# Linear attention in a four-layer kernel: the third layer sums keys with normalised rows over the tokens and applies the value weights to the sums

## The chip, the core and the metric

The kernel runs on one core of one Trainium2 chip. Its time is in device microseconds (us), the median of three runs. The core has five engines with an instruction queue each: TensorE (PE, matrix products; its weight loads are listed as PEld), VectorE (DVE), ScalarE (ACT), GpSimd (POOL) and SyncE (SP). They share a memory of 128 partitions on the chip. Matrix products end in PSUM, eight banks of 128 partitions x 512 float32. DMA moves data to and from DRAM; in this kernel SP issues all of them.

## What is computed

The input x has 2048 tokens of 576 numbers (bfloat16). Two kinds of layer alternate, A, B, A, B, each as x = x + layer(layernorm(x)):

```python
def _A_ref(x, wqkv, wo):                      # x is already normalised
    B, S, D = x.shape                         # 1, 2048, 576
    H = 32; Dh = D // H                       # 18
    qkv = (x @ wqkv).reshape(B, S, 3, H, Dh).transpose(2, 0, 3, 1, 4)
    q, k, v = qkv[0], qkv[1], qkv[2]
    phi = lambda t: jnp.where(t > 0, t + 1, jnp.exp(t)) + 1e-6
    pq, pk = phi(q), phi(k)
    kv = jnp.einsum("bhsd,bhse->bhde", pk, v)
    z = jnp.einsum("bhsd->bhd", pk)
    num = jnp.einsum("bhqd,bhde->bhqe", pq, kv)
    den = jnp.einsum("bhqd,bhd->bhq", pq, z)[..., None] + 1e-6
    return (num / den).transpose(0, 2, 1, 3).reshape(B, S, D) @ wo

def _B_ref(x, w1, b1, w2, b2):                # x is already normalised
    y = _layernorm(x)
    h = gelu(y @ w1 + b1)                     # 4608 hidden
    return h @ w2 + b2
```

The kernel normalises once ahead of each layer. Layer 3 is the second A; the change is made there.

## The kernel before

**Tiles.** A *token tile* t is 128 tokens (16 of them, `NT`); a *chunk* c is four token tiles (`TPC` = 4, `CA` = 512 tokens, four chunks). The 576 columns are cut into five pieces of 128 (`KD`, the last of 64) where they are contracted, into five groups g of seven heads (126, 126, 126, 126, 72; `GR`, offsets `GO`) where heads matter, and into two halves of 288 (`HALF`). `yT` holds the normalised rows transposed, the columns on the partitions, for all tokens.

**Buffers.** `ps_h` has four PSUM buffers of one bank that nearly everything rotates through (keys, queries, denominators, h of the MLP); `ps_acc` has two of two banks, tags `accA` and `accB`. `blk` has 36 buffers of 128 x 576 bfloat16 for keys, queries, the hidden blocks `hT` of the MLP and more; `rows` has nine for rows of x in float32. `v_ring` is a ring of two value tiles.

**Order.** A helper `pe()` (L141) chains the products of TensorE in the order of the program. The other engines' queues are laid out by a scheduler, which some calls bind with `add_manual_dep` (one instruction not before another on the same queue). `warm_pe(n)` (L174) issues n products over zeros at the start (n = 11 at L812, 2 more at L822), while the first rows of x arrive and are normalised.

**Rows on their way into layer 3.** Layer 2 is an MLP; for its last chunk (as for each) 36 blocks hT are multiplied with w2 for one token tile after the other (L790). After each tile `residual` (L448) adds the layer's input and stores x to DRAM (`x_d`), and `LNPipe` (L264) normalises the tile in steps, one step per call of `tick`. With `evac="dma"` the normalised tile y is turned by `turn_rows` (L227): VectorE transposes blocks of 32 x 32 into `turned`, and after the fourth tile of a chunk SP stores them to `y_d` in DRAM in four pieces. `land` (L242) loads the chunk from `y_d` into `yT` some ticks later.

**Layer 3, the loop over tokens** (`layer_A`, L472, with li = 2; loop at L538). For each token tile: `k_proj` (L478) makes two halves of keys, five products of 288 columns each, into `k_ps`. The first half goes through `phi_from_psum` (L416: exp and an identity pass with bias 1 on ScalarE, then min/add and max on VectorE), the second through `phi_by_dve` (L407: exp on ScalarE, the rest on VectorE). `v_proj` (L493) makes the values in ten products (252 and 324 columns), which ScalarE and VectorE copy into `v_ring`; a column of ones stands beside them. `kv_acc` (L516) multiplies keys and values of the tile before, per group, five products of 126 (once 72) columns that are summed over all tokens in one PSUM buffer (`kvacc`). From the third tile on, one `q_proj` (L527; five products of 512 columns, then phi) follows: 16 of the 20 pairs (g, chunk) of queries are made in A.

**Layer 3, after the loop.** The sums are masked per head into `kvT` (L557, L561); z comes from the row of ones with five small products (L567) and is spread into `zsel` (L569, L571). Then the order is written out (L635 to L676): `kv_wo(g)` (L576) multiplies kvT of a group with wo, two products of 288 columns, copied out by ScalarE for even g, by VectorE for odd g; `den_stage(c)` (L591) sums the denominators of a chunk and takes the reciprocal; `quad_stage(c)` (L606) masks it for four token tiles; `scale_stage(g, c)` (L615) broadcasts it with one product of 512 columns (`rden_ps`), copied by ScalarE (`rden_bc`) and multiplied into pq by VectorE (L620); `wo_stage(t)` (L623) makes the output of a token tile with ten products of 288 columns and adds the residual. The order is kv_wo(0), a query, den 0, den 1, two queries around kv_wo(1), three scales, kv_wo(2) and (3), two scales, kv_wo(4), the last query; then the loop over t with, between the output tiles, the scales of the next chunk and the denominators of the one after.

**Layer 2's end.** `LayerB.run` (L758) walks the chunks; the last chunk's last tile (t = 15) is where the hidden blocks in `blk` come free for the last time before layer 3. Layers 1 and 4 are not touched but for the start-up and some memory set in layer 1.

Of the kernel before, what the change touches and what calls it, by code (L numbers as in the profile page):

```python
# [20 lines left out]
G = 5  # L21
# [13 lines left out]
def build(tc, A_x, A_wqkv, A_wo, B_w1, B_b1, B_w2, B_b2, out, dbg=None, n_layers=4):  # L35
    nc = tc.nc
    dbg = dbg or {}
    with ExitStack() as ctx:
# [76 lines left out]
        x_d = dpool.tile([NT, P, D], F32, name="x_d")  # L115
        y_d = [dpool.tile([D // 32, 32, CB], BF16, name=f"y_d{i}") for i in range(2)]
# [109 lines left out]

        def turn_rows(y, t, kind):  # L227
# [14 lines left out]
        def land(now=False):  # L242

            for it in list(landing):
# [8 lines left out]
                for hi in range(2 if kind == "B" else 1):  # L253
                    nc.sync.dma_start(out=yT[64 * hi:64 * (hi + 1), KD - 1, cols],
                                      in_=home[16:18, :, :].rearrange("jj r n -> (jj r) n"))

# [7 lines left out]
        class LNPipe:  # L264
# [11 lines left out]
            def tick(self, transposes=1):  # L276
                land()
                for it in list(self.items):
# [61 lines left out]
                    elif st in (2, 3):  # L340
# [18 lines left out]
                        if it["kind"] == "B" and it["evac"] != "dma":  # L359
                            nc.gpsimd.tensor_copy(out=y[:, D:DPAD], in_=y[:, 4 * P:D])  # L360
                        it["y"] = y
# [54 lines left out]
        def phi_from_psum(ps_ap, out_ap, rows, n, turned_cols=False):  # L416
# [3 lines left out]
            if turned_cols:  # L420
                e_out, a_out, ps_ap = spread(e_out), spread(a_out), gather(ps_ap)
            act_last["exp"] = nc.scalar.activation(out=e_out, in_=ps_ap, func=ACT.Exp).ins.name  # L422
            act_last["phi"] = nc.scalar.activation(out=a_out, in_=ps_ap, func=ACT.Identity, bias=C1,
                                                   scale=1.0).ins.name
            nc.vector.tensor_scalar(out=e[0:rows, 0:n], in0=e[0:rows, 0:n], scalar1=1.0, scalar2=1e-6,
                                    op0=ALU.min, op1=ALU.add)
            top = nc.vector.tensor_tensor(out=out_ap, in0=a[0:rows, 0:n], in1=e[0:rows, 0:n], op=ALU.max)
            dve_last["phi"] = top.ins.name
# [43 lines left out]
        def layer_A(li, next_kind, pre_a1=None):  # L472
# [54 lines left out]
            def q_proj(g, c):  # L527
# [6 lines left out]
                phi_from_psum(qp[0:GR[g], :], pq[(g, c)][0:GR[g], 0:CA], GR[g], CA, turned_cols=(li > 0))  # L534
# [3 lines left out]
            for t in range(NT):  # L538
# [13 lines left out]
            q_proj(*q_left.pop(0))  # L552
            kv_acc(NT - 1)
            q_proj(*q_left.pop(0))

            kvacc = kvacc_of["ps"]
            nc.vector.tensor_tensor(  # L557
                out=kvT[0:127, 0:4, :].rearrange("p g (h e) -> p g h e", h=7),
                in0=kvacc[0:127, 0, 0:504].rearrange("p (g h e) -> p g h e", g=4, h=7),
                in1=maskz[0:127, :, :].unsqueeze(1).to_broadcast([127, 4, 7, DH]), op=ALU.mult)  # L560
            nc.vector.tensor_tensor(  # L561
                out=kvT[0:127, 4, 0:72].rearrange("p (h e) -> p h e", h=4),
                in0=kvacc[0:127, 1, 0:72].rearrange("p (h e) -> p h e", h=4),
                in1=maskz[0:127, 0:4, :], op=ALU.mult)
            zp = ps_h.tile([P, 512], F32, name="z_ps", tag="h")
            for g in range(G):
                pe(nc.tensor.matmul(zp[0:GR[g], g:g + 1], lhsT=kvT[0:127, g, 0:GR[g]], rhs=z_row[0:127, :],  # L567
                                 start=True, stop=True))
# [5 lines left out]
            kvwo = {}  # L574

            def kv_wo(g):  # L576
                wp = ps_acc.tile([P, 2, 512], F32, name="kvwo_ps", tag=("accB", "accA")[g % 2])
# [5 lines left out]
                if g % 2:  # L583
                    nc.vector.tensor_copy(out=out, in_=wp[0:GR[g], :, 0:HALF])
                else:
                    nc.scalar.copy(out=out, in_=wp[0:GR[g], :, 0:HALF])
# [4 lines left out]
            def den_stage(c):  # L591
# [10 lines left out]
                with nc.allow_low_precision("reciprocal of the denominator in the reference's bfloat16"):  # L602
                    nc.vector.reciprocal(out=rden[:], in_=dp[:, 0:P])
                rden_of[c] = rden

            def quad_stage(c, after=None):  # L606
# [6 lines left out]
                quad_rden[c] = quad  # L613

            def scale_stage(g, c):  # L615
# [4 lines left out]
                nc.vector.tensor_tensor(out=pq[(g, c)][0:GR[g], 0:CA], in0=pq[(g, c)][0:GR[g], 0:CA],  # L620
                                        in1=rb[0:GR[g], 0:CA], op=ALU.mult)
# [26 lines left out]
            for g in range(3):  # L648
                scale_stage(g, 0)
# [257 lines left out]
```

## Time and profile before

| what | value |
| --- | --- |
| median of three runs | 774.79 us (774.26 to 775.12) |
| the profiled execution | 775.07 us, of it span 773.4 us |
| granted TensorE clock over the span | 1.00 |
| DMA, mean over the span | 88 GB/s; 30.0% of the engines' time |
| layer 3: first key product to end of output | 390.56 to 488.38 us |

The span runs from the first to the last instruction on the core. Costliest in layer 3 are the groups below: the line, engine, operation, output <- inputs, shapes and count; then the busy time in all, the mean duration of one in ns, and the idle time of the engine just before them with what ended it.

| group, 390.56 to 488.38 us | busy us | mean ns |
| --- | --- | --- |
| L530 PE q_ps, 512 columns, x100 | 25.0 | 382 |
| L484 PE k_ps, 288 columns, x160 | 22.2 | 286 |
| L628 PE wo_ps, 288 columns, x160 | 22.0 | 286 |
| L503 PE v_ps, 324 columns, x80 | 13.6 | 300 |
| L500 PE v_ps, 252 columns, x80 | 11.2 | 271 |
| L524 PE kvacc, 126 columns (and 72), x80 | 6.8 | 214 |
| L422 ACT exp of q_ps, x20 | 11.9 | 596 |
| L505 ACT copy v_ring<-v_ps, x16 | 9.3 | 579 |
| L620 DVE pq<-pq,rden_bc, x20 | 8.0 | 420 |
| L603 DVE reciprocal rden<-den_ps, x4 | 3.8 | 953 |

The duration of a product runs from its start to its modelled end, with the drain; consecutive products overlap, so durations add up to more than the time they take, and the step from start to start is the price of one more.

### The profile page before, as it was taken

The page shows a single profiled execution, that of the slowest core. Times are in us where ns is not written, and L with a number is a line of the kernel's source. Part 1 is how long each engine was busy: PE and PEld are TensorE (multiplying, and loading weights), DVE is VectorE, ACT ScalarE, POOL GpSimd, SP SyncE. Part 2 cuts the span into 40 slices and gives each one's busy share as a digit, 9 for nine tenths or more (in the row PEclk, how much of TensorE's full clock was granted, in tenths as well). Part 3 has the DMA queues.
Part 4 walks back from the last instruction along what each step waited for, and adds up shares of the span by engine and source line. Part 5 has one row for each costly group of instructions (what it writes and reads, how often), then busy time and mean ns, then how long its engine had stood idle before and what let it go on. Part 6 is the DMA issues. An engine that isn't in the chain of part 4 may idle for free.

```text
span 773.4 us, 15771 instructions
## 1 busy us (share of the span) xinstructions
PE 764.4 (99%) x6611; PEld 495.4 (64%) x6611; DVE 272.1 (35%) x685; ACT 345.4 (45%) x765; POOL 118.2 (15%) x191
## 2 busy tenths in 40 slices
PE   9999999999999999999999999999999999999998
PEld 6776664675477457646777766547745764675476
DVE  7786864036013503401355578520140032000000
ACT  5887946304610650264046677561065026304600
POOL 4571412013000301200100004110030012002000
PEclk9999999999999999999999999999999999999999
DMA  8991473016301710320440005830141033011000
GB/s 266 265 291 45 151 254 87 22 59 169 83 16 47 200 50 32 90 66 16 139 108 2 1 2 165 296 81 8 32 129 53 16 124 81 8 32 54 1 9 23
DMA packets 73761, 69.10 MB, mean 89 GB/s; under 512 B 34266, under 2 KB 58330, under 8 KB 73690
## 3 DMA queue, kind: packets, MB, share of 16 engines
q1 hardware_dynamic: 73690, 68.10, 30.0%
q8 instruction: 51, 0.84, 0.4%
q14 instruction: 20, 0.16, 0.1%
HBM read 45.67 MB, written 22.41 MB: 88 GB/s over the span
## 4 chain that ended last, share of the span: by engine, by line
PE 94%; DVE 2%; ACT 1%; DMA 1%; issue 1%; POOL 1%; SPq 0%; POOLq 0%; ACTq 0%; DVEq 0%
PE m_ps L790 35%; PE h_ps L736 20%; PE hp_ps L736 16%; PE q_ps L530 6%; PE k_ps L484 4%; PE wo_ps L628 3%; PE v_ps L503 2%; PE v_ps L500 2%; PE m_half L790 1%; PE kvacc L524 1%; PE tp L379 1%; PE rden_ps L617 1%; DMA x<-in_A_x_dram 1%; ACT rden_bc L619 1%; DMA xo<-x_d 0%
## 5 line engine op out<-in xcount | busy, mean ns | idle before, releaser
L790 PE MATMUL m_ps<-w_sb,hT 128*128 128x288 bf16 x2232 | 274.8, 286 | 0.0
L790 PEld LDWEIGHTS <-hT 128*128 128x128 bf16 x2304 | 224.8, 98 | 59.8 <-issue 3.4
L736 PEld LDWEIGHTS <-w_sb 64*128 64x128 bf16 x2304 | 124.6, 94 | 136.5 <-issue 1.9
L736 PE MATMUL hp_ps<-yT,w_sb 64*128 64x512 bf16 x1152 | 178.0, 376 | 0.0
L736 PE MATMUL h_ps<-yT,w_sb 64*128 64x512 bf16 x1152 | 148.0, 376 | 0.0
L741 ACT COPY relay_sb<-relay_sb 128x1 f32<-128x1 f32 x144 | 28.6, 198 | 262.3 <-PE h_ps L736 220.0
L732 ACT ACTIVATE hT<-h_ps,b1T 128x512 bf16<-128x512 f32 x144 | 91.1, 684 | 44.4 <-PE h_ps L736 44.4
L333 POOL TENSOR_TENSOR ln_rstd<-ln_u,neg_half 128x1 f32<-128x1 f32 x64 | 36.4, 570 | 385.0 <-DVE ln_u L324 241.1
L732 ACT ACTIVATE hT<-hp_ps,b1T 128x512 bf16<-128x512 f32 x144 | 91.2, 693 | 0.0
L462 DVE TENSOR_TENSOR xbf<-m_ps,xo 128x576 bf16<-128x576 f32 x15 | 11.4, 758 | 211.7 <-PE m_ps L790 211.7
L462 DVE TENSOR_TENSOR xo<-m_ps,xo 128x576 f32<-128x576 f32 x16 | 12.1, 758 | 178.5 <-PE m_ps L790 178.5
L445 POOL TENSOR_TENSOR xo<-xo,b_bc 128x576 f32<-128x576 f32 x32 | 40.9, 1282 | 101.6 <-DMA xo<-x_d 61.3
L736 PE MATMUL h_ps<-yT,w_tail 64*128 64x512 bf16 x144 | 54.1, 376 | 0.0
L736 PE MATMUL hp_ps<-yT,w_tail 64*128 64x512 bf16 x144 | 54.1, 376 | 0.0
L530 PE MATMUL q_ps<-yT,wqkv_sb 128*126 128x512 bf16 (+1 forms) x200 | 50.0, 382 | 0.0
L628 PE MATMUL wo_ps<-kvwo,pq 126*128 126x288 bf16 (+1 forms) x320 | 43.7, 286 | 1.1 <-DVE pq L620 1.1
L484 PE MATMUL k_ps<-wqkv_sb,yT 128*128 128x288 bf16 x320 | 44.6, 286 | 0.2
L484 PEld LDWEIGHTS <-yT 128*128 128x128 bf16 x320 | 31.0, 98 | 12.2 <-ACT yT L382 0.8
L736 PEld LDWEIGHTS <-w_tail 64*128 64x128 bf16 x288 | 27.1, 94 | 17.1
L628 PEld LDWEIGHTS <-pq 126*128 126x128 bf16 (+1 forms) x320 | 30.3, 97 | 12.0 <-DVE pq L620 2.0
L422 ACT ACTIVATE phi_e<-k_ps 128x288 bf16<-128x288 f32 x46 | 19.3, 419 | 35.3 <-PE k_ps L484 34.9
L422 ACT ACTIVATE phi_e<-q_ps 126x512 bf16<-126x512 f32 (+1 forms) x40 | 23.9, 596 | 23.3 <-PE q_ps L530 22.9
(109 smaller groups left out, 648.2 us busy)
## 6 DMA issues: line engine op xcount, KB each, us to landing
xo<-x_d SPq DMA_DIRECT2D x48, 288.0 KB, 3.9
x_d<-xo SPq DMA_DIRECT2D x32, 288.0 KB, 2.1
xl<-x_d SPq DMA_DIRECT2D x24, 288.0 KB, 4.3
y_d<-turned SPq DMA_DIRECT2D x40, 144.0 KB, 3.2
w_sb<-in_B_w_dram SPq DMA_DIRECT2D x6, 864.0 KB, 10.1
yT<-y_d SPq DMA_DIRECT2D x10, 512.0 KB, 4.1
w_sb<-in_B_w_dram SPq DMA_DIRECT2D x9, 512.0 KB, 5.6
x_d<-xn SPq DMA_DIRECT2D x16, 288.0 KB, 2.6
```

The source lines that it names most:

```text
L333: nc.gpsimd.tensor_tensor(out=rstd[:], in0=it["u"][:], in1=neg_half[:], op=ALU.pow)
L422: act_last["exp"] = nc.scalar.activation(out=e_out, in_=ps_ap, func=ACT.Exp).ins.name
L445: nc.gpsimd.tensor_tensor(out=xo[:], in0=xo[:], in1=b2_bc[:], op=ALU.add)
L462: total = nc.vector.tensor_tensor(out=xn[:, cols].rearrange("p (h n) -> p h n", h=2), in0=halves, in1=xo[:, cols].rearrange("p (h n) -> p ...
L484: pe(nc.tensor.matmul(kp[:, 0:HALF], lhsT=yT[:, k, tok], rhs=wqkv_sb[:, k, D + half * HALF: D + (half + 1) * HALF], start=(k == 0), stop=( ...
L500: pe(nc.tensor.matmul(vp[:, 0, 0:252], lhsT=yT[:, k, tok], rhs=wqkv_sb[:, k, 2 * D: 2 * D + 252], start=(k == 0), stop=(k == KD - 1)))
L530: pe(nc.tensor.matmul(qp[0:GR[g], :], lhsT=wqkv_sb[:, k, GO[g]:GO[g] + GR[g]], rhs=yT[:, k, c * CA:(c + 1) * CA], start=(k == 0), stop=(k ...
L628: pe(nc.tensor.matmul(wp[:, half, 0:HALF], lhsT=pq[(g, c)][0:GR[g], j * P:(j + 1) * P], rhs=kvwo[g][0:GR[g], half * HALF:(half + 1) * HALF ...
L732: act_last["gelu"] = nc.scalar.activation(out=to, in_=ps, func=ACT.Gelu_apprx_tanh, bias=b1T[:, f:f + 1], scale=1.0).ins.name
L736: mm = pe(nc.tensor.matmul(dst[n], lhsT=wt, rhs=mv, start=(seen[n] == 0), stop=(seen[n] == 8)))
L741: relay = nc.scalar.copy(out=relay_sb[:, 1:2], in_=relay_sb[:, 0:1])
L790: pe(nc.tensor.matmul(acc[half][:, 0:HALF], lhsT=hT[f][:, j * P:(j + 1) * P], rhs=w2_sb[:, f, half * HALF:(half + 1) * HALF], start=(f == ...
```

## The change

In layer 3 the order of two products is exchanged. Before, values v = y wv are made for each token tile (y the normalised rows), and the keys are summed with them: phi(k)^T v. After, the normalised rows themselves are summed with the keys over all tokens, y^T phi(k), a matrix of 576 x 576, and the value weights are applied once to this sum: wv^T (y^T phi(k)), of which only the blocks on the diagonal, per group of heads, are made. Layer 1 keeps the old way.

- **Rows.** The products need the rows with the tokens on the partitions. SP stores each normalised tile to DRAM (`yrow_d`) when it is made, and loads it again (`load_row`, 128 x 512 into a `blk` buffer): twelve tiles ahead of the last tile of layer 2's MLP, the last four in `land` after the last `yT`. The last 64 columns (the *tail*) go into the memory of `v_ring`, 65 columns per tile, the last a column of ones set once in layer 1 (`tail_ones`); so the sum's 65th row of the tail is z.
- **Two passes.** The sums of 576 x 288 for one key half take five PSUM banks: `accA`, `accB` (two each) and one of the four buffers of `ps_h` for the tail (`k2_tail`). So the loop over the tokens runs twice, once for each key half: `k_half` makes the keys of the half, `rows_by_keys` follows three steps later (`LAG`), five products of 288 columns each, and a `q_proj` comes after every second step. At the end of a pass the sums are copied as bfloat16 into five tiles `k2`, three parts by ScalarE and two by VectorE.
- **Value weights.** `kv_groups` makes the diagonal blocks, five products for each group, and masks them into `kvT`. Groups 0 and 1 come in the second pass (t = 6), their `kv_wo` in four halves at t = 8 to 11; groups 2 to 4 come after the loop.
- **z** is taken from the 65th row of `k2[4]` with a column of `ident`.
- **The bridge** (from z to the first output): three queries instead of four; two of them, and the first one's last VectorE step, are bound behind other work (`after`, `dve_after`, `defer`); `den_stage(1)` moves behind the last kv_wo; kv_wo(2) is copied out by VectorE, as kv_wo(3) is; kv_wo(4) uses the other accumulator. One query is left for the output loop.
- **Start-up:** `warm_pe(9)` instead of 11.

The diff, cut:

```diff
+        yrow_d = dpool.tile([NCB, TPC, 4, 32, D], BF16, name="yrow_d")
...
+        def tail_of(t):
+            flat = v_ring[t // 8][:].rearrange("p g c -> p (g c)")
+            return flat[:, (t % 8) * 65:(t % 8 + 1) * 65]
+        def tails(c):
+            flat = v_ring[c // 2][:].rearrange("p g c -> p (g c)")
+            return flat[:, (c % 2) * 260:(c % 2 + 1) * 260].rearrange("p (t e) -> p t e", e=65)
+        def tail_ones():
+            for c in range(NCB):
+                nc.gpsimd.memset(tails(c)[:, :, 64:65], 1.0)
...
+        def load_row(t):
+            row_of[t] = blk.tile([P, D], BF16, name="yrow", tag="blk")
+            nc.sync.dma_start(out=row_of[t][:, 0:4 * P], in_=yrow_d[t // TPC, :, t % TPC, :, 0:4 * P])
...
+                if kind == "A":
+                    for i in range(4):
+                        nc.sync.dma_start(out=tails(c)[:, i, 0:64], in_=yrow_d[c, :, i, :, 4 * P:D])
+                    if c == NCB - 1:
+                        for t in range(c * TPC, NT):
+                            load_row(t)
...
+                        if it["kind"] == "A" and it["evac"] == "dma":
+                            c, j = divmod(it["t"], TPC)
+                            nc.sync.dma_start(out=yrow_d[c, j].rearrange("i r d -> (i r) d"), in_=y[:, 0:D])
...
+            if after is not None:
+                for step in (exp, ident_pass):
+                    tc.add_manual_dep(step.ins, after, NOSYNC, reason="broadcasts first")
...
+            if dve_after is not None:
+                tc.add_manual_dep(top.ins, dve_after, NOSYNC, reason="denominators first")
...
+            if li > 0:
+                self_k = dict(pk={}, acc=None, rows={})
+                k2 = [blk.tile([P, D], BF16, name="k2", tag="blk") for _ in range(KD)]
+                nc.gpsimd.memset(k2[4][64:P, :], 0.0)
+                def k_half(t, half):
+                    kp = ps_h.tile([P, 512], F32, name="k_ps", tag="h")
+                    for k in range(KD):
+                        pe(nc.tensor.matmul(kp[:, 0:HALF], lhsT=yT[:, k, t * P:(t + 1) * P],
+                                            rhs=wqkv_sb[:, k, D + half * HALF: D + (half + 1) * HALF],
+                                            start=(k == 0), stop=(k == KD - 1)))
+                    if t % 2 == 0:
+                        self_k["pk"][(half, t // 2)] = blk.tile([P, D], BF16, name="pk", tag="blk")
+                    pk = self_k["pk"][(half, t // 2)][:, (t % 2) * HALF:(t % 2 + 1) * HALF]
+                    (phi_by_dve if half else phi_from_psum)(kp[:, 0:HALF], pk, P, HALF)
+                def rows_by_keys(t, half):
+                    if t == 0:
+                        self_k["acc"] = [ps_acc.tile([P, 2, 512], F32, name="k2_ps", tag=tag) for tag in ("accA", "accB")]
+                        self_k["tail"] = ps_h.tile([P, 512], F32, name="k2_tail", tag="h")
...
+                    for k in (4, 0, 1, 2, 3):
+                        dst = self_k["tail"][0:65, 0:HALF] if k == 4 else self_k["acc"][k // 2][:, k % 2, 0:HALF]
+                        lhsT = tail_of(t) if k == 4 else row_of[t][:, k * P:(k + 1) * P]
+                        pe(nc.tensor.matmul(dst, lhsT=lhsT, rhs=pk, start=(t == 0), stop=(t == NT - 1)))
...
+                    cols = slice(half * HALF, (half + 1) * HALF)
+                    nc.scalar.copy(out=k2[4][0:65, cols], in_=self_k["tail"][0:65, 0:HALF])
+                    for i, copy in enumerate((nc.scalar.copy, nc.vector.tensor_copy)):
+                        for j in range(2):
+                            copy(out=k2[2 * i + j][:, cols], in_=self_k["acc"][i][:, j, 0:HALF])
+                def kv_groups(groups):
+                    ps = ps_h.tile([P, 512], F32, name="kv_ps", tag="h")
...
+                    for g in groups:
+                        cols = slice(GO[g], GO[g] + GR[g])
+                        for k in range(KD):
+                            pe(nc.tensor.matmul(ps[0:GR[g], GO[g] - base:GO[g] - base + GR[g]],
+                                                lhsT=wqkv_sb[:, k, 2 * D + GO[g]:2 * D + GO[g] + GR[g]],
+                                                rhs=k2[k][:, cols], start=(g == groups[0] and k == 0), stop=(k == KD - 1),
+                                                skip_group_check=True))
...
+                def kv_wo_half(g, half):
+                    wp = ps_h.tile([P, 512], F32, name="kvwo_half", tag="h")
+                    pe(nc.tensor.matmul(wp[0:GR[g], 0:HALF], lhsT=kvT[0:GR[g], g, 0:GR[g]],
+                                        rhs=wo_sb[0:GR[g], g, half * HALF:(half + 1) * HALF], start=True, stop=True))
...
+                    copy = nc.vector.tensor_copy if half else nc.scalar.copy
+                    copy(out=kvwo[g][0:GR[g], half * HALF:(half + 1) * HALF], in_=wp[0:GR[g], 0:HALF])
+                LAG = 3
+                steps = [(t, half) for half in range(2) for t in range(NT)]
+                behind = []
+                for n, (t, half) in enumerate(steps):
+                    pre_a1(t)
+                    k_half(t, half)
+                    behind.append((t, half))
+                    if n % 2 == 1:
+                        q_proj(*q_left.pop(0))
+                    if len(behind) > LAG:
+                        rows_by_keys(*behind.pop(0))
+                    if half and t == 6:
+                        kv_groups((0, 1))
+                    if half and t in (8, 9, 10, 11):
+                        kv_wo_half((t - 8) // 2, t % 2)
+                while behind:
+                    rows_by_keys(*behind.pop(0))
+                zp = ps_h.tile([P, 512], F32, name="z_ps", tag="h")
+                for g in range(G):
+                    pe(nc.tensor.matmul(zp[0:GR[g], g:g + 1], lhsT=k2[4][:, GO[g]:GO[g] + GR[g]], rhs=ident[:, 64:65],
+                                        start=True, stop=True))
+            for t in range(NT) if li == 0 else ():
...
-            q_proj(*q_left.pop(0))
-            kv_acc(NT - 1)
-            q_proj(*q_left.pop(0))
...
+            if li == 0:
+                q_proj(*q_left.pop(0))
+                kv_acc(NT - 1)
+                q_proj(*q_left.pop(0))
+                zp = kv_from_sums()
...
             def kv_wo(g):
-                wp = ps_acc.tile([P, 2, 512], F32, name="kvwo_ps", tag=("accB", "accA")[g % 2])
+                wp = ps_acc.tile([P, 2, 512], F32, name="kvwo_ps", tag=("accB", "accA")[(g + (g == 4 and li > 0)) % 2])
...
-                if g % 2:
+                if g % 2 or (li > 0 and g == 2):
                     nc.vector.tensor_copy(out=out, in_=wp[0:GR[g], :, 0:HALF])
                 else:
-                    nc.scalar.copy(out=out, in_=wp[0:GR[g], :, 0:HALF])
+                    act_last["kvwo"] = nc.scalar.copy(out=out, in_=wp[0:GR[g], :, 0:HALF]).ins.name
...
                                         start=False, stop=True))
...
-                    nc.vector.reciprocal(out=rden[:], in_=dp[:, 0:P])
+                    recip = nc.vector.reciprocal(out=rden[:], in_=dp[:, 0:P])
+                if after is not None:
+                    tc.add_manual_dep(recip.ins, after, NOSYNC, reason="first products first")
...
+            else:
+                phi = q_proj(*q_left.pop(0), defer=True)
+                den_stage(0)
+                quad_stage(0)
+                phi(dve_after=dve_last["quad"])
+                kv_groups((2, 3, 4))
+                late = [q_proj(*q_left.pop(0), defer=True)]
+                for g in range(3):
+                    scale_stage(g, 0)
+                kv_wo(2)
+                kv_wo(3)
+                late.append(q_proj(*q_left.pop(0), defer=True))
+                for g in range(3, G):
+                    scale_stage(g, 0)
+                kv_wo(4)
+                den_stage(1, after=dve_last["mult"])
+                quad_stage(1, after=dve_last["mult"])
+                for phi in late:
+                    phi(after=act_last["kvwo"])
...
                     for j in range(TPC):
...
+                        if next_kind == "A" and t == NT - 1:
+                            for row in range(NT - TPC):
+                                load_row(row)
...
-        warm_pe(11)
+        warm_pe(9)
...
+                if li == 0 and n_layers > 2:
+                    tail_ones()
             else:
                 pe_chain.update(on=True)
                 lbs[li].run()
```

## The prediction

> **What bounds the kernel now.** I read the busy shares first, then the chain of waits, then three stretches of layer 3.
>
> ```profile
> PE 764.4 (99%) x6611; PEld 495.4 (64%) x6611; DVE 272.1 (35%) x685; ACT 345.4 (45%) x765; POOL 118.2 (15%) x191
> ...
> PE 94%; DVE 2%; ACT 1%; DMA 1%; issue 1%; POOL 1%; SPq 0%; POOLq 0%; ACTq 0%; DVEq 0%
> ```
>
> TensorE is busy for 99% of the span and holds 94% of the chain that ended last, so a matmul taken out of a full stretch is time gained, and work moved to other engines is free where TensorE does not wait for it.
>
> ```profile
> core 0: us, PE busy (x) PEld busy (x) DVE busy (x) ACT busy (x) POOL busy (x), PEclk, DMA share, GB/s
> 390.56:451.80 61.24, 61.14 (x483) 45.68 (x480) 34.76 (x118) 40.38 (x94) 0.55 (x1) 1.00 0.12 30
> 451.80:461.50 9.70, 8.41 (x90) 5.21 (x90) 8.52 (x24) 8.25 (x16) 0.00 (x0) 1.00 0.00 0
> 461.50:488.38 26.88, 25.81 (x245) 18.41 (x244) 20.29 (x37) 19.04 (x40) 9.01 (x20) 1.00 0.55 178
> ```
>
> I call them A, B and C. A is the loop over tokens, from the first key matmul of layer 3 to the first z_ps: TensorE never rests, VectorE and ScalarE are 57% and 66% busy. B is the bridge from z_ps to the first wo_ps; VectorE and ScalarE are as loaded as TensorE there. C is the output projection. Together 97.82 us.
>
> What one token costs in A is read from the chain in order of time (start, us, what):
>
> ```profile
> 446.93 0.54 PE v_ps L500 x5
> 447.47 0.69 PE v_ps L503 x5
> 448.15 0.26 PE kvacc L524 x5
> ```
>
> and from the step between two matmuls on TensorE (start to start; the durations of a page row also hold the drain): 288 columns 122 ns, 512 columns 216 ns, 126 columns 57 ns (kvacc, and the five z_ps with 126-wide weights, also 57), 72 columns 31 to 35 ns.
>
> **A, the sums.** Removed for each of 16 tokens: v_ps, 0.54 + 0.69 = 1.23 us, and kvacc, 0.26. Added: ten row products of 288 columns (five in each key half), 10 x 0.122 = 1.22 us. Rows for values is an exchange; kvacc is the gain: 16 x 0.26 = 4.2 us. The key products (10 x 0.122 a token) and the 16 query products in A (5 x 0.216 = 1.08 each) stay. The value weights come back once, as 25 small products: 20 x 57 + 5 x 35 ns = 1.3 us, ten of them (0.57) in A and 15 (0.75) in B. Four of the ten kvwo products (4 x 0.122 = 0.49) move from B to A. At its end z_ps now waits for the ScalarE copy of the 65-row tail: the tail product is issued first of its five, so it ends about 0.2 before the next step would, and a copy like the exp (0.42) puts z_ps 0.15 to 0.2 late. A becomes 61.24 - 4.2 + 0.57 + 0.49 + 0.15 = 58.2 (57.9 to 58.6).
>
> The Trainium skill (TensorE: Matmul & The Clock Gate, Back-to-back issue gap) states about 81 ns for a sustained pair of weight load and matmul of 128 columns. The trace differs: kvacc steps at 57 ns. By the page the 25 products would take 2.0 us and the gain be 0.7 smaller.
>
> The evictions of A: v_ps needed a ScalarE pass (0.58) and a VectorE pass (0.23) a token; they go. ScalarE gets three passes over a key half in pairs of steps, as now, and one more in the first pass: a pair of steps is 2 x 0.61 key, 2 x 0.61 rows, 1.08 query = 3.5 us of TensorE against 4 x 0.29 + 0.49 + 0.48 = 2.1 us of ScalarE starts. VectorE has about 2 us. Both stay covered by TensorE; were that cover gone, the price is the rival "pinch" below.
>
> **B, the bridge.** TensorE's own work in B now is 0.29 (z) + 4 x 1.08 (queries) + 10 x 0.122 (kvwo) + 2 x 0.34 (den) + 5 x 0.216 (rden) = 7.6, so 2.1 us of its 9.70 are waits. After: 0.29 + 3 x 1.08 + 0.75 + 0.68 + 1.08 + 6 x 0.122 = 6.8. I laid out the three queues in the changed order. VectorE copies two quarters of the sums (about 0.4 each, like the 288-wide key passes), makes zsel, then reciprocal 0.95, the mask product of kvT and quad 0.41, so the first rden_ps waits 0.4 to 0.6; the last kvwo product waits for the second of two 0.75 us kvwo copies that stand among three pq products on VectorE (0.6 to 0.8); the first wo_ps waits for the ScalarE copy of that product, since both use one accumulator (0.5). Waits 1.7 to 2.3, sum 8.5 to 9.1; I take 8.8.
>
> **C, the output.** One query product (1.08) moves into it. With it VectorE gets two more query evictions (starts 0.18 + 0.34 each), a reciprocal (0.87) and a quad (0.40): 2.3 us in the first part of C, which has no room:
>
> ```profile
> 469.59 0.91 PE L628 MATMUL wo_ps<-kvwo,pq 72*128 72x288 bf16 x6 [0.86 <-DVE pq L620]
> ```
>
> Here TensorE already waits 0.86 for a pq product of VectorE. 8.09 us after the start of C this matmul runs. Laid out with the new queue (reciprocal, two query evictions, quad, first residual 0.75, two pq products, and so on) it runs 9.1 to 9.6 after it. Behind it the order is the same as now, and VectorE has slack (6.6 us idle in C, nearly all later). C becomes 26.88 + 1.3 = 28.2. Bounds: 1.08 alone if VectorE keeps up (27.9, or 27.5 if the query fills the waits of C that exist now), and 1.08 + 1.2, the whole VectorE surplus (29.2).
>
> **Queues.** SP now also issues 16 row stores, 16 row loads and 16 tail loads. The stores wait for VectorE's norm, so what stands behind them on SP (the residual loads of layers 2 and 3) waits with them; those lie in layer 2's MLP and have tens of us. The first twelve row loads wait, one by one, for matmuls of the last m_ps token (381.6 to 390.6) whose hT buffers they take, and for DMAs eight places back; with 3 to 4 us each (y_d 3.2, xl 4.3) they are in by about 390, and the first is read some 4.6 us after the start of A. The last four, the tail loads and the last quarter of yT come after it:
>
> ```profile
> 396.24 2.85 SPq L238 DMA_DIRECT2D y_d<-turned  x4
> ...
> 402.04 0.38 SPq L251 DMA_DIRECT2D yT<-y_d  x1
> ```
>
> yT landed at 402.04 + 4.1 (median of that transfer) = 406.1, and was wanted at 434.3, at the key product of token 12. Now the first pass wants it after 12 key halves, 6 queries and 9 row products: 390.56 + 7.3 + 6.5 + 5.5 = 409.9. The cover shrinks from 28 us to 3.8, but holds: nothing. POOL's clearing of one buffer (about 0.3) stands ahead of a 0.55 rstd there, inside this cover. The ones in v_ring are set in layer 1, off the path.
>
> **Start.** Two warm-up products of 0.43 us go. The chain there runs through the third x row (landed 7.58) and VectorE's statistics, not through them, so no gain. In the changed order VectorE's copy of the second yT stands one 0.2 us instruction later: between 0 and +0.3. If the slow start-up step (427 ns against 216 for 512 columns) lasted through the first key products, 10 x 0.12 more, half of it hidden: +0.7 at most. I take +0.1.
>
> **The sum.** 58.2 + 8.8 + 28.2 = 95.2 against 97.82, and +0.1: 2.5 us faster. The profiled execution took 775.07 us (span 773.4), 0.28 above the median of 774.79: 772.6 by its own time, 772.3 for the median. With all bounds on one side, A 57.9, B 8.5, C 27.5 give 3.9 less, 58.6 + 9.1 + 29.2 and +0.7 give 0.2 less; the likeliest one's own range is 771.2 to 773.2.
>
> **Rivals.**
> Pinch. The tail sum occupies one of the four buffers that keys and queries rotate through for a whole pass, so three are left. In the second pass a query product waits for VectorE's last step on the key half before it: 0.17 drain + 0.43 exp + 0.23 + 0.46 = 1.3 us against 1.34 of work between (row products, one kvwo, one key half). With 0.1 us lost in each of 16 pairs, 1.6 is gone: 773.9. For it: the near equality; against: only two or three pairs are so tight, the others have 1.8 or more.
> The Trainium skill (Perfetto Trace Analysis, Identifying Performance Opportunities) says that the same gap repeating on the engine that should be saturated can mean too few buffers; before, TensorE rests 0.10 us in all of A.
>
> Bridge closes. The queries set aside fill the waits of B and C, VectorE never decides: A 57.9, B 8.2, C 27.5 is 4.2 less: 770.6. For it: ScalarE loses 16 v_ring copies and the reciprocals are spaced out; against: the 0.86 wait.
>
> Late last quarter (slower). The y_d stores, the four tail loads (in 128-byte pieces), yT and four row loads share SP's queue, eight in flight. TensorE waits for yT at token 12 once it lands after 409.9, and the kernel is slower than before once it lands after about 414. If both hops took twice their medians (y_d 3.2, yT 4.1), yT would land at 396.24 + 2.85 + 6.4 + 8.2 = 413.7, and with the tails' four issues ahead of it (4 x 0.4) at 415.3: 5.4 us lost, 777.7. For it: the cover shrinks sevenfold; against: the DMA share there is 0.7 at most, and the longest landing of a y_d store was 5.0.
>
> **Chances.** Forecast 0.50, pinch 0.20, bridge closes 0.17, late last quarter 0.13. A measurement of this kernel tells about 0.2%, 1.55 us, from no change: below 773.2 is faster, above 776.3 slower. Forecast and bridge are faster (0.67), pinch is within (0.20), late is slower (0.13). The range leaves out the late case and the edge of the bridge: 770.2 to 774.8.
>
> **What would show it.** Right: no kvacc or v_ps rows in layer 3, row products stepping at 122 ns, the first z_ps some 58 us after the first key product, TensorE without gaps in the two passes, the first wo_ps about 8.8 us after z_ps, C longer than before by about 1.3. Wrong: gaps before q_ps in the second pass (pinch), a wait on yT or a row load before k_ps (late), a longer wait of wo_ps on pq than 1.5 us, or steps of the 126-column products near 81 ns.

## The result and the profile after

The changed kernel takes 778.38 us (median of four runs, 778.0 to 779.85) against 774.57 us before: 1.0052 times as long, with a 95% interval of 1.0035 to 1.0069. It is slower, and outside the predicted range. The profiled execution took 778.17 us, of it a span of 776.4 us.

The page, with the busy shares and the chain that ended last, by engine:

```profile
PE 762.0 (98%) x6549; PEld 492.9 (63%) x6554; DVE 273.9 (35%) x676; ACT 339.7 (44%) x755; POOL 118.9 (15%) x196
...
PE 95%; DVE 1%; DMA 1%; ACT 1%; SPq 1%; issue 0%; DVEq 0%; ACTq 0%
```

This looks like before: TensorE is busy 98% of the span. The lost time doesn't show in shares over the whole kernel. The three stretches of layer 3 show it (us, then busy time and count by engine, granted clock, DMA share, GB/s):

```profile
core 0: us, PE busy (x) PEld busy (x) DVE busy (x) ACT busy (x) POOL busy (x), PEclk, DMA share, GB/s
389.93:455.08 65.15, 59.54 (x417) 43.93 (x414) 35.11 (x109) 36.77 (x86) 0.70 (x1) 0.95 0.22 63
455.08:463.89 8.81, 7.71 (x96) 4.80 (x95) 6.68 (x18) 5.09 (x12) 0.00 (x0) 1.00 0.01 2
463.89:491.47 27.58, 26.66 (x246) 18.96 (x248) 22.30 (x42) 20.26 (x43) 8.92 (x20) 1.00 0.68 224
```

A, the loop over tokens, took 65.15 us where 61.24 were before and 58.2 were predicted; B took 8.81 (9.70 before, 8.8 predicted), C 27.58 (26.88 before, 28.2 predicted). Outside layer 3 only the start moved: the first product of layer 2 came 0.64 us earlier. The sum is -0.64 + 3.91 - 0.89 + 0.70 = 3.1 us, the 3.0 between the spans. So the change won time in B, lost some in C, and in A something took about 7 us that the sums of products don't hold: PE was idle for 5.61 of the 65.15 us, and the clock was 0.95. The list of waits names the idle part (engine, line, what it waited for: us in all, times, longest):

```profile
PE k_ps L585 <- DMA yT<-y_d: 5.6, 1, 5.6
```

One wait, at 409.4 us, before the first key product of token 12, for the last quarter of yT. Around it, as stretches of time in the columns of the view above:

```profile
409.43:411.70 2.27, 0.00 (x0) 0.00 (x0) 0.72 (x2) 0.51 (x2) 0.00 (x0) 1.00 0.30 50
411.70:415.04 3.34, 0.00 (x0) 0.00 (x1) 0.00 (x0) 0.00 (x0) 0.00 (x0) 0.50 0.68 198
415.04:418.57 3.53, 3.53 (x16) 2.31 (x16) 0.54 (x2) 0.71 (x2) 0.00 (x0) 0.51 0.27 86
418.57:424.00 5.43, 5.43 (x39) 3.98 (x38) 2.35 (x8) 3.84 (x10) 0.00 (x0) 1.00 0.10 33
```

TensorE rested from 409.43 to 415.04. The granted clock fell to 0.50 at 411.7, in the middle of the rest, and stayed there until 418.5, so the first 15 products afterwards took 3.53 us instead of 15 x 0.1225 = 1.84. The rest cost 5.8 us (from the start of the last product before it to the start of the first one after it, beyond a normal step), the slow clock 1.7, together 7.5. Without them A would be 57.7 us, and the three stretches together 94.1 instead of 97.82: 3.7 us less than before.

The loop itself runs as forecast. One half step of it in the chain (start, us, what): the tail product, four row products and the next five key products, 0.122 us each.

```profile
394.70 0.12 PE k_tail L602
394.82 0.49 PE k_ps L602 x4
395.31 0.61 PE k_ps L585 x5
```

Why yT is late is read from SP's queue (start, us from the first issue of a group to the end of its last, what, count):

```profile
383.35 12.24 SPq L245 DMA_DIRECT2D yrow<-yrow_d  x10
395.68 1.24 SPq L389 DMA_DIRECT2D yrow_d<-y_ring  x1
396.97 0.42 SPq L476 DMA_DIRECT2D xo<-x_d  x1
397.49 0.39 SPq L503 DMA_DIRECT2D x_d<-xo  x1
...
404.69 0.32 SPq L476 DMA_DIRECT2D xo<-x_d  x1
405.10 2.58 SPq L258 DMA_DIRECT2D y_d<-turned  x4
407.79 3.02 SPq L278 DMA_DIRECT2D v_ring<-yrow_d  x4
410.98 0.38 SPq L271 DMA_DIRECT2D yT<-y_d  x1
```

Ten row loads hold SP for 12.24 us. The x store of token 15 is issued at 397.49, where SP's queue before the change has

```profile
391.59 0.32 SPq L469 DMA_DIRECT2D x_d<-xo  x1
```

Then the next residual load waits 6.2 us, until 404.69:

```profile
SPq L476 <- DMA x_d<-xo: 6.2, 1, 6.2
```

It reuses the buffer that the x store reads, and that store took from 397.49 to 404.67 to land (x_d stores of this kind: 2.1 us in the median, before). The landings in the trace show what held it: twelve of the sixteen engines that carried it were done by 402.45, the other four only between 404.21 and 404.67. Each of the row loads ahead of it was carried by four engines, and they landed one after another, from the fourth on 1.4 to 1.7 us apart, between 385.85 and 402.84. The four y_d stores stand behind that load and are issued at 405.10, 8.9 us later than before; the last of their rows had been turned at 395.06. yT follows at 410.98 and lands at 415.0. The key product of token 12 wanted it at 409.3, a step after the product before it. No product waited for a row load itself.

### The profile page after: what moved, and what is told of

Read it like the earlier page. It is cut to its first block, busy times and chain, and to the rows that moved or that the text cites. A ratio compares the mean times of both kernels' runs of the same rounds, so it can differ in the third digit from the quotient of the medians.

```text
span 776.4 us, 15723 instructions
## 1 busy us (share of the span) xinstructions
PE 762.0 (98%) x6549; PEld 492.9 (63%) x6554; DVE 273.9 (35%) x676; ACT 339.7 (44%) x755; POOL 118.9 (15%) x196
## 4 chain that ended last, share of the span: by engine, by line
PE 95%; DVE 1%; DMA 1%; ACT 1%; SPq 1%; issue 0%; DVEq 0%; ACTq 0%
PE m_ps L949 35%; PE h_ps L892 20%; PE hp_ps L892 16%; PE q_ps L564 5%; PE wo_ps L764 4%; PE k_ps L518 2%; PE k_ps L585 2%; PE k_ps L602 2%; PE v_ps L537 1%; PE m_half L949 1%; PE v_ps L534 1%; PE tp L408 1%; PE rden_ps L752 1%; DMA wqkv_sb<-in_A_wqkv_dram 1%; PE kvacc L558 1%; DMA yT<-y_d 1%
## 5 line engine op out<-in xcount | busy, mean ns | idle before, releaser
L457 DVE TENSOR_SCALAR phi_e<-phi_e 128x288 bf16<-128x288 bf16 (+2 forms) x86 | 24.6, 287 | 30.2 <-ACT phi_e L451 29.8
L564 PEld LDWEIGHTS <-wqkv_sb 128*126 128x126 bf16 (+1 forms) x200 | 24.9, 132 | 11.7
```

Source lines behind the costliest of these rows:

```text
L564: pe(nc.tensor.matmul(qp[0:GR[g], :], lhsT=wqkv_sb[:, k, GO[g]:GO[g] + GR[g]], rhs=yT[:, k, c * CA:(c + 1) * CA], start=(k == 0), stop=(k ...
```

## The experiments

My theory after this: the row loads themselves are slow, since each reads four groups of 32 rows (32 rows of each of a chunk's four stored tiles, the order of the tokens in yT) and is served by four DMA engines only; they hold SP, and what is queued behind them is late twice. The rivals: the traffic as such, the four tail loads ahead of yT (the prediction's late case), or the loads disturbing TensorE in another way.

### Row loads of 128 rows that follow each other

```diff
-yrow_d = dpool.tile([NCB, TPC, 4, 32, D], BF16, name="yrow_d")
+yrow_d = dpool.tile([NCB, 4, TPC, 32, D], BF16, name="yrow_d")
...
-    in_=yrow_d[t // TPC, :, t % TPC, :, 0:4 * P]
+    in_=yrow_d[t // TPC, t % TPC].rearrange("j r d -> (j r) d")[:, 0:4 * P]
...
-    out=yrow_d[c, j].rearrange("i r d -> (i r) d")
+    out=yrow_d[c, :, j]
```

The tail loads change in the same way. The four groups don't vanish: a row store now writes them, where it wrote 128 rows that follow each other.

> The rows in DRAM are laid out so that one row load reads 128 rows that follow each other, instead of four groups of 32; sizes, number and places of all transfers stay. Theory (a row load in four groups runs on four of the sixteen DMA engines, some 95 packets of 1 KB per us; SP is held at their issue until 395.6 and the x store behind them lands late): the twelve loads issue in about 0.5 us each, y_d issues by 397 to 398, yT lands before 409.4, the 5.6 us wait and the slow clock after it are gone, 770.5 to 771.5 us. Rival (the amount of traffic, or the issue of so many transfers, makes yT late whatever their shape): the wait stays above 4 us, 777 to 778.5 us.

Measured: 771.48 us (771.39 to 771.59), 0.9954 of before (0.9940 to 0.9969). The same bytes, in another order in DRAM, turn a loss of 0.5% into a gain of 0.5%. SP's queue in this run:

```profile
383.83 4.71 SPq L245 DMA_DIRECT2D yrow<-yrow_d  x10
...
391.81 0.32 SPq L503 DMA_DIRECT2D x_d<-xo  x1
...
396.19 3.65 SPq L258 DMA_DIRECT2D y_d<-turned  x4
399.93 2.78 SPq L278 DMA_DIRECT2D v_ring<-yrow_d  x4
403.22 0.37 SPq L271 DMA_DIRECT2D yT<-y_d  x1
```

Ten loads take 4.71 us instead of 12.24, the x store is issued at 391.81, the y_d stores at 396.19, and yT at 403.22. TensorE doesn't wait for yT, and the three stretches are

```profile
390.79:448.47 57.68, 57.68 (x416) 43.21 (x414) 35.12 (x109) 36.76 (x86) 0.69 (x1) 1.00 0.20 52
448.47:457.29 8.82, 7.72 (x97) 4.81 (x95) 6.69 (x18) 5.10 (x12) 0.00 (x0) 1.00 0.01 2
457.29:484.86 27.57, 26.65 (x246) 18.96 (x248) 22.29 (x42) 20.25 (x43) 8.92 (x20) 1.00 0.67 226
```

A is 57.68 us with PE busy for all of it at a clock of 1.00: the 65.15 less the 7.5 above. The theory holds; the rival that traffic decides falls. The last two row stores, now in four groups, took 4.6 and 4.3 us to land, and nothing on the path waited for them.

How many engines serve a load is seen in the DMA share while row loads run. One stretch of the changed kernel, with row loads alone, and one of this run, with an x store among them until 386.0:

```profile
390.00:395.50 5.50, 5.50 (x39) 4.02 (x38) 4.93 (x16) 3.52 (x10) 0.70 (x1) 1.00 0.27 92
```

```profile
384.00:388.00 4.00, 4.00 (x35) 3.19 (x34) 1.58 (x4) 0.00 (x0) 1.12 (x2) 1.00 0.85 253
```

A share of 0.27 of 16 engines is 4.3 engines, at 92 GB/s; 0.85 is 13.6 engines, at 253 GB/s; from 386.1 to 388.6, with row loads alone, this run has 0.94 (15 engines) and 283 GB/s. The Trainium skill (DMA: Bandwidth & Descriptors, "Why a DMA increments its semaphore by 16 and not by 1") states that a transfer is split over the largest number of engines up to 16 that divides the size of the slowest dimension on both sides: 4 and 128 give four here, 128 and 128 give 16. The trace agrees: besides the shares, it marks the landing of a row load once for each engine, four times in the changed kernel and sixteen times here.

### Eight groups

```diff
-yrow_d = dpool.tile([NCB, TPC, 4, 32, D], BF16, name="yrow_d")
+yrow_d = dpool.tile([NCB, 4, 2 * TPC, 17, D], BF16, name="yrow_d")
...
-    in_=yrow_d[t // TPC, :, t % TPC, :, 0:4 * P]
+    in_=yrow_d[t // TPC, t % TPC, :, 0:16, 0:4 * P]
...
-nc.sync.dma_start(out=yrow_d[c, j].rearrange("i r d -> (i r) d"), in_=y[:, 0:D])
+for i in range(4):
+    nc.sync.dma_start(out=yrow_d[c, i, 2 * j:2 * j + 2, 0:16, :], in_=y[32 * i:32 * i + 32, 0:D])
```

The 17th row of each group is never used; it keeps the groups apart. The tail loads read the same groups.

> The changed kernel with rows laid out so that a row load reads eight groups of 16 rows (a store is then four transfers of 32 rows). Theory (the number of groups is the number of DMA engines that serve a load, four at a time and 95 packets per us with four groups): eight at a time, 170 to 190 packets per us, a load in 0.7 us, SP free of them by 391, y_d issues by 399, no wait or one under 1 us, 771.3 to 773 us. Rival (any load that isn't one run of rows is slow): some 95 packets per us again, the wait of over 4 us stays, 777 to 780 us.

Measured: 771.45 us (771.30 to 771.56), 0.9955 of before (0.9940 to 0.9970). While row loads run:

```profile
387.00:391.50 4.50, 4.50 (x39) 3.59 (x38) 0.58 (x1) 0.00 (x0) 0.00 (x0) 1.00 0.53 178
```

0.53 x 16 = 8.5 engines and 178 GB/s, twice the four groups, and each row load's landing is marked eight times. So it is the number of groups that sets the rate, and not whether the rows follow each other. Eight groups are enough here: yT is issued at 405.61 and no wait appears.

### The residual loads behind yT

```diff
 load = nc.sync.dma_start(out=xo[:], in_=x_d[t])
+behind_yT = li > 0 and not add_b2 and "yT" in state
+if behind_yT:
+    tc.add_manual_dep(load.ins, state["yT"], NOSYNC, reason="residual rows behind yT")
```

`state["yT"]` is the last load of yT, in this and the next kernel. The slow loads stay.

> The loads of layer 3's residual rows stand behind yT on SP; the row loads keep their four groups. Theory of a blocked head (the second residual load waits 6.2 us for the x store to land and holds the y_d stores behind it): y_d issues at 398.4 instead of 405.1, yT lands at 407 to 409.5, the wait is 0 to 0.5, 770.5 to 772 us. Rival (the four DMA engines are full until about 402, and y_d's packets queue behind the row loads there, whatever SP does): y_d issues early but lands as late as 406 to 407, the wait is still 2 to 4 us, 774 to 776.5 us.

Measured: 772.44 us (771.92 to 773.12), 0.9967 of before (0.9954 to 0.9980), 0.4 above the range of the theory.

```profile
384.07 11.87 SPq L245 DMA_DIRECT2D yrow<-yrow_d  x10
...
398.34 5.16 SPq L258 DMA_DIRECT2D y_d<-turned  x4
404.64 2.18 SPq L278 DMA_DIRECT2D v_ring<-yrow_d  x4
406.99 0.38 SPq L271 DMA_DIRECT2D yT<-y_d  x1
```

The row loads hold SP as long as before, but y_d is issued at 398.34 and yT at 406.99. Of the wait for yT, 5.61 us in the changed kernel, 0.85 is left:

```profile
PE k_ps L588 <- DMA yT<-y_d: 0.9, 1, 0.9
```

So 4.8 us of the wait came from the y_d stores standing behind a load that waited for the x store. The rest is put down to the four engines still being full: the four y_d stores took 5.16 us to issue here, 2.85 before, and twelve engines had done their part of the last one at 405.46, the other four at 406.42. That the tail loads, issued until 406.82, added to it is not ruled out.

### The tail loads behind yT

```diff
 tail = nc.sync.dma_start(out=tails(c)[:, i, 0:64], in_=yrow_d[c, :, i, :, 4 * P:D])
+tc.add_manual_dep(tail.ins, state["yT"], NOSYNC, reason="tails behind yT")
...
-load_row(t)
+load_row(t, after=tail.ins.name)
```

The second part keeps the last four row loads behind the tails, as they were.

> The four tail loads of each chunk stand behind yT on SP instead of ahead of it; nothing else moves. Theory (the row loads decide; yT has to wait for the y_d stores to land in any case, which is at about 410): yT issues at most 1 us earlier, the wait shrinks from 5.6 to about 4.7, 777 to 778 us. Rival (the tails' four issues, 3.0 us ahead of yT, are the price, as in the prediction's late case): yT issues at about 408, the wait is 2.6, 774.5 to 775.5 us.

Measured: 779.01 us (778.27 to 780.0), 1.0052 of before (1.0037 to 1.0067): no gain, and above the theory's 777 to 778. The wait is 5.48 us, where 4.7 was expected. In the chain of the changed kernel the tail loads had stood directly ahead of yT; with them gone the chain goes through the landing of y_d (start, us, what):

```profile
407.53 4.05 DMA y_d<-turned
...
411.70 4.00 DMA yT<-y_d
```

yT has to wait for y_d anyway, and that was hidden below the tails' issue: in the changed kernel the last y_d store landed at 410.58, and the tails' issue ended at 410.81. A step of the chain is not a price: another wait lay under it. The 0.1 us less of wait is too little for the runs to show (those of the changed kernel go from 778.0 to 779.85), and in the profiled execution the clock outweighed it:

```profile
410.27:414.64 4.37, 0.00 (x0) 0.00 (x0) 0.72 (x2) 0.51 (x2) 0.00 (x0) 1.00 0.41 116
414.64:415.75 1.11, 0.00 (x1) 0.01 (x1) 0.00 (x0) 0.00 (x0) 0.00 (x0) 0.50 0.59 153
415.75:421.47 5.72, 5.72 (x21) 3.46 (x22) 1.09 (x4) 1.42 (x4) 0.00 (x0) 0.50 0.25 80
```

Here it fell 4.4 us after the last product, not 2.3, and was low for the first 5.72 us of work instead of 3.53. At the full clock these products (15 of 288 columns, five of 512) take 2.9 us, so the slow clock cost 2.8 us here and 1.7 there.

### Filling the rest with products

```diff
 kp = ps_h.tile([P, 512], F32, name="k_ps", tag="h")
+for _ in range(22 if (t, half) == (12, 0) else 0):
+    pe(nc.tensor.matmul(kp[:], lhsT=wqkv_sb[:, 0, 0:P], rhs=wqkv_sb[:, 0, 0:512], start=True, stop=True))
```

> Adds 22 products of 512 columns, whose result is overwritten, ahead of the first key product of token 12 in the first pass (22 x 0.216 = 4.75 us of the 5.6 us wait). Theory (the 3 us of half-speed products after the wait come from TensorE having rested; they cost 1.8 us): the granted clock stays 1.00, yT lands as late as before, 776.3 to 776.9 us. Rival (the slow products come from something else, so the clock drops anyway): no change, 778 to 778.6 us.

Measured: 776.93 us (776.17 to 777.25), 1.0023 of before (1.0013 to 1.0033), where the changed kernel has 1.0052: 0.0029 of 775, 2.2 us, by the ratios, 1.45 by the medians. That is the upper end of the theory's 776.3 to 776.9; the rival had 778 to 778.6. The clock is 1.00 all through. TensorE around yT's landing (one of the 22 products has no record):

```profile
410.37 4.91 PE L585 MATMUL k_ps<-wqkv_sb 128*128 128x512 bf16 x21
415.62 0.79 PE L587 MATMUL k_ps<-wqkv_sb,yT 128*128 128x288 bf16 x5 [0.34 <-DMA yT<-y_d]
```

The wait for yT now ends a filled stretch, and the five key products after it run in 0.79 us. Useless work made the kernel faster: the slow clock was a cost of the rest, 1.45 to 2.2 us by the runs and 1.7 by the steps.

### The loads in the kernel before

```diff
+nc.sync.dma_start(out=yrow_d[c, j].rearrange("i r d -> (i r) d"), in_=y[:, 0:D])
...
+if next_kind == "A" and t == NT - 1:
+    for row in range(NT - TPC):
+        load_row(row)
```

> The kernel before, with the change's 16 row stores and its twelve row loads in four groups at the same place; the loaded rows are not used, the arithmetic is that of before. Theory (the loads make yT late in any kernel; what costs time is that the two passes ask for it at 409 instead of 434): the y_d stores issue 6 to 10 us later than before, yT lands at 411 to 416, and no wait appears before a key product: 774.3 to 775.5 us, as before. Rival (the loads disturb TensorE by themselves, through buffers of the hidden blocks or the chip's memory): a wait of over 1 us in layer 3 or at the end of layer 2, over 776 us.

Measured: 775.02 us (774.36 to 775.53), 1.0002 of before (0.9993 to 1.0011).

```profile
383.73 11.93 SPq L230 DMA_DIRECT2D yrow<-yrow_d  x10
...
404.87 0.32 SPq L450 DMA_DIRECT2D xo<-x_d  x1
405.28 2.50 SPq L243 DMA_DIRECT2D y_d<-turned  x4
410.44 0.39 SPq L256 DMA_DIRECT2D yT<-y_d  x1
```

SP's queue is as disturbed as in the changed kernel, y_d leaves 9.0 us late, yT is issued at 410.44 instead of 402.04, and nothing happens: A, B and C are 61.24, 9.70 and 26.88 as before. The late yT costs time only because two passes ask for it at 409 instead of 434.

### Two warm-up products fewer in the kernel before

```diff
-warm_pe(11)
+warm_pe(9)
```

> The kernel before with 9 warm-up products instead of 11. Theory (the start hangs on the first loads and on VectorE, as the prediction has it; the first key product at 6.35 in the profile of after, against 7.07, was that run's luck, since four other runs with 9 had 7.09 to 7.45): no change, 774.3 to 775.5 us, first key product between 6.3 and 7.5. Rival (the two products stand ahead of the first transposes): 0.6 to 0.8 us faster, 773.7 to 774.2 us, in every run.

Measured: 774.90 us (774.34 to 775.26), 1.0001 of before (0.9992 to 1.0010). The first key product came at 7.18 us (7.07 with 11, 6.35 in the changed kernel's run). In the profiles of the seven edited versions of the changed kernel, all with 9, it came at 6.72 to 7.45. So the 0.64 us that the profile after showed at the start doesn't come from two products fewer; it is put down to the scatter of executions.

### All three moves together

The wide loads, the tail loads and the residual loads behind yT, with the edits above.

> Row loads of 128 rows that follow each other, tail loads behind yT, residual loads behind yT, all three together. Theory (once yT lands before 409.4 nothing of the queue is on the path): the same as with the wide loads alone, 771 to 772 us, yT landing some 3 us earlier without use. Rival (something of SP's queue still costs): 0.5 us or more below the wide loads alone.

Measured: 771.69 us (771.53 to 771.87), 0.9958 of before (0.9944 to 0.9972). yT is issued at 402.05, 1.2 us before the wide loads alone (some 3 were expected), without use: A is 57.69. Once yT is in time, the rest of SP's order makes no difference that the runs show.

### One copy back to ScalarE

The wide loads, and the copy of kv_wo(2) on ScalarE again. The waits left in the bridge and after it, with the wide loads alone:

```profile
456.16 0.41 PE L711 MATMUL kvwo_ps<-wo_sb,kvT 72*72 72x288 bf16 x2 [0.70 <-DVE kvwo L716]
...
457.29 1.39 PE L764 MATMUL wo_ps<-kvwo,pq 126*128 126x288 bf16 x10 [0.27 <-ACT kvwo L718]
...
466.44 0.79 PE L764 MATMUL wo_ps<-kvwo,pq 72*128 72x288 bf16 x5 [0.81 <-DVE pq L755]
```

```diff
-if g % 2 or (li > 0 and g == 2):
+if g % 2:
     nc.vector.tensor_copy(out=out, in_=wp[0:GR[g], :, 0:HALF])
```

> The wide loads, and kv_wo(2) copied out by ScalarE (as before the change) instead of VectorE. Theory (the 0.70 us that the last kvwo product waits is the second of two 0.75 us copies on VectorE behind pq products; ScalarE rests for 0.66 us at that point, about one copy of 0.67): the wait falls to 0 to 0.2 and the bridge from 8.82 to 8.1 to 8.4, 770.8 to 771.3 us. Rival (ScalarE's broadcast copies come later by the copy, and with them the pq products; the wait moves to a rden_ps or to the first wo_ps): bridge 8.7 to 9.2, 771.3 to 771.9 us.

Measured: 770.74 us (770.32 to 771.29), 0.9947 of before (0.9933 to 0.9961). The bridge:

```profile
448.40:456.86 8.46, 7.64 (x96) 4.89 (x95) 6.18 (x17) 5.54 (x13) 0.00 (x0) 1.00 0.01 2
```

8.46 us against 8.82: the 0.70 is gone, but 0.20 appear before den_ps, which waits for a broadcast copy of ScalarE, and the wait of the first wo_ps, for ScalarE's copy of kv_wo(4), grows from 0.27 to 0.49. So 0.36 of the 0.70 is won, between the theory (a bridge of 8.1 to 8.4) and the rival (8.7 to 9.2), whose later copies are seen. A and C are those of the wide loads, 57.69 and 27.57. The median is the lowest of the study, but its interval overlaps that of the wide loads (0.9940 to 0.9969), so the gain is shown by the bridge of one profile, not by the times.

## Why the prediction was wrong

**The step that failed** is in "Queues": that the first twelve row loads, "with 3 to 4 us each", are "in by about 390", and that yT's landing at 406.1 therefore doesn't move: "The cover shrinks from 28 us to 3.8, but holds: nothing". The 3 to 4 us were landing times of y_d and xl. A landing time is no rate: twelve loads that use the same four engines follow one another at 92 GB/s, which is 1.4 us for 128 KB, and the last landed at 402.84. SP was held until 395.6, and two things behind it were late: the x store, and the y_d stores, which stood behind a load that waits for that store. So yT landed at 415.0 instead of 406.1, and the term put at nothing was 5.8 us of rest and 1.7 of slow clock. The prediction gave the row loads a landing time, the tails alone an issue time on SP, and saw that stores and loads share the queue, but did not follow which old instruction stood behind the new ones, and for what it waited. The wide loads undo it: 771.48, where 772.3 was forecast.

**The late case** was among the rivals and priced at 777.7, close to the 778.38. Its point of decision was right (wanted at 409.9; measured 409.3), and so was its place. That its landing of 415.3 is near the measured 415.0 is luck, as its mechanism was not right: moving the tails won nothing, and what grew was not the hops of y_d and yT (from the first issue of y_d to that of yT 5.8 us before and 5.9 after) but the time before y_d was issued. It got 0.13 since "the DMA share there is 0.7 at most" and the longest y_d store took 5.0; a mean share of 16 engines says nothing of four that are full. The price also left out the slow clock after the rest, 1.7 us in that profile.

**A** was right in its mechanism. The kvacc products, 4.18 us from start to start, went; the row products took the place of the value products (320 products of 288 columns for keys and rows in 39.35 us, where keys and values took 39.48); ten kv products took 0.57 and four kvwo halves 0.51. Without the stall it is 57.7, just under the forecast of 58.2 (57.9 to 58.6): the wait at z_ps, put at 0.15, didn't come, and the query products stepped 0.3 us less in all.

**B** came out at the 8.8 that was forecast, with an error in the sum. Its three waits, 0.4 to 0.6, 0.6 to 0.8 and 0.5, add up to 1.5 to 1.9, not to the 1.7 to 2.3 that it wrote, so its own terms give 8.3 to 8.7. Measured from start to start beyond a normal step, as it counted, the waits with the wide loads were 0.29 for rden_ps, 0.86 for the last kvwo product and 0.46 for the first wo_ps, 1.6 together (as idle time 0.13, 0.70 and 0.27). The places were right. The other 7.2 us are TensorE's own work, put at 6.8: small gaps between groups of products that no term held.

**C** was mis-sized: +0.69 where 1.3 was forecast. The wait on a pq product stayed, 0.81 us for 0.86, at 9.16 us after the start of C (9.1 to 9.6 forecast); so VectorE's surplus stayed hidden, only the query product's 1.08 came in, and 0.4 of it went into waits that had existed before (from start to start 1.55 us of them before, 1.13 with the wide loads). It was the lower bound, 27.5.

**The start** was right in saying that two warm-ups win nothing.

**The pinch** didn't occur: PE was busy for 57.68 of 57.68 us in A with the wide loads, with three buffers to rotate through.

**The kv products** stepped at 57 ns, as the rows of before said: ten in 0.57 us.

## What to carry to other kernels

Before a transfer is priced, look at the slowest dimension of both of its sides: in the runs here it set how many engines served it, four, eight or sixteen. A layout in DRAM that made it 128 for the loads moved the four groups to the stores, off the path, and cost nothing. When transfers are added to a queue, list the old ones that come behind them, what each waits for, and how long its user can wait; here 28 us of cover had become 4 by the same edit that filled the queue. And a rest of TensorE of 5.5 to 5.6 us cost 1.7 to 2.8 us more than its length, one of 0.85 us did not, so a late input is worth filling or moving even when it can't be removed.

## What the runs showed of the hardware that was not expected

- A row load in four groups ran at 92 GB/s, in eight at 178, in one run of 128 rows at 283, with DMA shares of 0.27, 0.53 and 0.94.
- With the engines of a narrow load full, the issue itself gets slow on SP: ten loads in 12.24 us, against 4.71 us with wide loads. And a wide transfer behind narrow ones waits for them: the x store landed after 7.2 us instead of 2.1; twelve of its engines were done by 402.45, the other four at 404.21 to 404.67.
- The granted clock fell to half 2.3 us after the last product in one run and 4.4 us in another, and came back 6.8 us later in both (411.7 to 418.5 and 414.6 to 421.5). What it costs depends on how much of those 6.8 us is work: 3.53 and 5.72 us here, which lost 1.7 and 2.8 us. In the run with a rest of 0.85 us it stayed at 1.00. The Trainium skill (TensorE: Matmul & The Clock Gate, "Part 1: The HAM clock gate") gives an idle window of about 3.4 us, which runs freely, before the clock falls. The 4.4 us fit that; the 2.3 us are shorter than a whole window of rest, so here the measurement differs from the page.
